# A scan and a two-level expert layer on one core: new ranks for the planner, four weight loads behind the first row load, and three groups of products moved forward

## The chip, the cores and the metric

The kernel runs on one core of one Trainium2 chip. The metric is the device time of one execution in microseconds (us); the time given is the median of three runs. One execution was profiled as well. TensorE is called PE here, VectorE DVE, ScalarE ACT, GpSimd POOL and SyncE SP, as in the profile.

## The reference

The input is 4 sequences of 3648 tokens with 256 channels, 14592 tokens in all. A gated scan runs over each sequence, then each token goes to one of 16 experts, chosen in two levels of 4.

```python
f = lower + (1 - lower) * sigmoid(f_logit)
for t in range(3648):                  # per sequence and channel
    h = f[:, t] * h + (1 - f[:, t]) * x[:, t]
    y[:, t] = h
g = argmax(y @ w_group)                # 4 groups;  g_w = softmax weight of g
e = argmax(y @ w_expert[g])            # 4 experts; e_w = softmax weight of e
out = g_w * e_w * (relu(y @ w1[g, e]) @ w2[g, e])   # 256 -> 1024 -> 256
```

Each token's result is written to its own row of the output.

## The kernel before, in words

**Stages.** The tokens are cut into 29 units of at most 512. A unit's inputs come by one DMA (L499). ACT makes the gates (`tanh` L520, `gate` L530), DVE the inflow (L536) and the scan (L552, one per half `k` of the channels, in order of the units). PE then does three things with the scanned `h`: the router's logits (`router` L608), their turn (`turn` L619), and the rows of the tokens (`back` L562 transposes `h`, ACT takes the high half in L569, `rows_rest` L591 subtracts it on PE, ACT takes the low half in L597). ACT also copies the router's result (`router_out` L614, `logits` L627). 15 groups of one or two units (`GROUPS`) are routed on DVE (L638 to L705) with a few small matmuls on PE (L672 to L689). POOL then scatters the rows, 128 tokens per instruction (L721), into the table `xs`, each expert's rows together.

**Jobs.** 32 jobs do the expert layers: 16 early ones (`EARLY`) on tokens of the first groups, and 16 later ones (`CAPS`) when all ranks are known. A job loads its rows transposed (`job_rows` L944, DMA from `xs` to `x`) and its meta rows (L935, L937), both by SP's queue. Its weights come in four pieces of 512 KB (`job_weights` L953). In the first four jobs (`f2` true) pieces 2 and 3 go straight into their tiles `w2`, `w3`; other pieces go through `st` and are cast by ACT (L959) and DVE (L962). The first products (`m1_mm` L980 to L982) come in groups: for job 0, which has one chunk of 320 columns, eight groups of six matmuls, each group in one PSUM buffer. ACT's relu (L997) empties it; in the first four jobs all groups use the ring `m1` of three buffers (`M1_BUFS`, `TWO_RINGS`). The second product is L1026, its scaling ACT L1037 and DVE L1045, and the way out POOL L1051. A last loop (L1333) takes what is left over.

Job 0 takes rows of groups 0 to 2, that is of 5 units or 20 scatters. Its row load waits until these have landed.

**What sets the order.** The order is not written out. Every step is a task of `Plan` with a key, a cost and the buffers that it takes. `Plan.add` adds to the key a rank out of the table `DELTA`, chosen by a letter and a number: `m3` is the first product of job 3, `r4` the router of unit 4, and so on:

```python
more = float(DELTA.get("%s%d" % self.tag, 0)) if self.tag else 0.0
t.key = key + more
```

`Plan.order` simulates the engines with these keys and returns the list `todo`. A few tasks are moved in the list afterwards, and the program issues the list as it stands, each engine taking its own instructions in that order:

```python
with tc.manual_schedule(engines={ET.SP, ET.PE, ET.DVE, ET.Activation, ET.Pool}):
    for t in todo:
        done = t.fn()
```

So an instruction that waits holds up all that is behind it on its own engine.

Of the kernel before, what the change touches and what calls it, by code (L numbers as in the profile page):

```python
# [49 lines left out]
L_UNIT = 90000.0  # L50
L_RT = 40000.0
L_LOW = 0.0
DELTA = {"B0": -517950, "B8": 43800, "b0": -360450, "b1": -398850, "b2": -500200, "b3": -96200, "b4": -83850, "b5":
# [47 lines left out]
ZX_WAIT = 99000.0  # L101
L_SCAN = 14000.0
L_ZX = 4000.0
# [11 lines left out]
X_BUFS = 5  # L115
HS_BUFS = 2
ROWS_FIRST = 3
BLANKS_FROM = 50000.0
BLANKS_AHEAD = 12000.0

# [176 lines left out]
def gated_scan_moe(ctx: ExitStack, tc, zx, lower, wroute, wexp, out, S):  # L297
# [811 lines left out]
    for g, G in groups.items():  # L1109
        T = G["T"]  # L1110
        key = need[g]
# [136 lines left out]
    tables = A("DVE", 3500, leftovers, after=[put], key=jobs[-13].at)  # L1248
    regs["left"] = None

    for n, j in enumerate(jobs):
        base = j.at
        dep = [T1[member[EARLY[j.nth][1]]]] if j.kind == "A" else [put]
# [3 lines left out]
        for i in range(4):  # L1257
# [3 lines left out]
                   new=[(f"w{i}", n) if i > 1 and j.f2 else ("st", n, i)], size=570000, wait=d - AHEAD)  # L1261
            if i > 1 and j.f2:
                halves[i] = [ld]
                continue
            plan.tag = "p", n
            ha = []
# [16 lines left out]
        for ch in range(len(j.chunks)):  # L1283
            w = j.cw[ch] + j.pad[ch]
            xs_of[ch] = [A("SP", max(1250.0, 15.6 * w / 4), lambda j=j, ch=ch, n=n: job_meta(j) if n < ROWS_FIRST and ch == 0 else job_rows(j, ch),
                          after=rows_dep, key=j.s1[ch] - L_ROWS,
                           new=[("x", n, ch)], size=36000 + int(1550 * w))]
        for ch, (t0, m) in enumerate(j.chunks):
            w = j.cw[ch]
            hb, xb = ("hh", n, ch), ("x", n, ch)  # L1290
# [2 lines left out]
            for cs in j.cols[ch]:  # L1293
                d = j.s1[ch] + cs[0]
                pb = (j.bank[ch, cs[0]], n, ch, cs[0])
                plan.tag = "m", n
                mm = A("PE", len(cs) * 6 * max(w / 2.4 + 2.4, 66.0), lambda j=j, ch=ch, cs=cs: m1_mm(j, ch, cs),
                       after=xs_of[ch] + halves[0] + halves[1], key=d, use=[xb] + wuse, new=[pb])
                hi = A("ACT", 80 + 0.83 * len(cs) * w, lambda j=j, ch=ch, cs=cs: m1_hi(j, ch, cs), after=[mm, firsth], key=d,
                       use=[pb] + ([hb] if firsth else []), new=[] if firsth else [hb])  # L1300
                firsth = firsth or hi
                hidden += [hi, None if j.f2 else A("DVE", 60 + 1.06 * len(cs) * w, lambda j=j, ch=ch, cs=cs: m1_lo(j, ch, cs), after=[hi], key=d,
                                 use=[pb, hb])]
# [14 lines left out]
    for b in [leads[8]] + [t for _, t in commons]:  # L1318
        if b.at > BLANKS_FROM:
            todo.remove(b)  # L1320
            todo.insert(next(i for i, t in enumerate(todo) if t.at >= b.at - BLANKS_AHEAD), b)
    with tc.manual_schedule(engines={ET.SP, ET.PE, ET.DVE, ET.Activation, ET.Pool}):
        for t in todo:
            done = t.fn()
# [76 lines left out]
```

## Time and profile before

| | |
|---|---|
| median of three runs | 729.41 us (727.68 to 730.82) |
| the profiled execution | 728.0 us, span 726.2 us |
| granted TensorE clock, mean of the span | 0.974 |
| PE busy | 689.4 us (95% of the span) |
| DVE, ACT, POOL busy | 506.2 us, 438.8 us, 286.2 us |
| moved by DMA | 151.53 MB, mean 209 GB/s |

The span runs from the first to the last instruction of the profiled execution, and its own time is 1.8 us more. The times of the rows below are counted from the span's start. The granted clock is a share of 2.4 GHz: 0.50 is the level of 1.2 GHz, 1.00 that of 2.4 GHz. PE's matmuls overlap, so the start of one to the start of the next is what it takes; the "us" of a row is from its first start to its last end. A matmul in fp32 leaves two records, so the eight fp32 matmuls of one unit's router stand as sixteen.

### The profile page before, as it was taken

The page shows a single profiled execution, that of the slowest core. Times are in us where ns is not written, and L with a number is a line of the kernel's source. Part 1 is how long each engine was busy: PE and PEld are TensorE (multiplying, and loading weights), DVE is VectorE, ACT ScalarE, POOL GpSimd, SP SyncE. Part 2 cuts the span into 40 slices and gives each one's busy share as a digit, 9 for nine tenths or more (in the row PEclk, how much of TensorE's full clock was granted, in tenths as well). Part 3 has the DMA queues.
Part 4 walks back from the last instruction along what each step waited for, and adds up shares of the span by engine and source line. Part 5 has one row for each costly group of instructions (what it writes and reads, how often), then busy time and mean ns, then how long its engine had stood idle before and what let it go on. Part 6 is the DMA issues. An engine that isn't in the chain of part 4 may idle for free.

```text
span 726.2 us, 17266 instructions
## 1 busy us (share of the span) xinstructions
PE 689.4 (95%) x6480; PEld 570.3 (79%) x6480; DVE 506.2 (70%) x1036; ACT 438.8 (60%) x875; POOL 286.2 (39%) x272
## 2 busy tenths in 40 slices
PE   3757999999999999999999999999999999999995
PEld 1435778788778887887888888899888988888994
DVE  6999599898999968864965532343854427768583
ACT  6987978767795567555445532434654336647572
POOL 1277377676167546472512212222222122143223
PEclk9956999999999999999999999999999999999998
DMA  8899999998988998998388442062767625763750
GB/s 333 315 333 311 341 322 311 305 273 250 346 295 182 322 271 173 243 336 130 94 210 229 142 98 58 30 177 63 183 168 194 142 56 157 225 195 97 266 147 24
DMA packets 133676, 151.53 MB, mean 209 GB/s; under 512 B 103928, under 2 KB 104505, under 8 KB 130263
## 3 DMA queue, kind: packets, MB, share of 16 engines
q1 hardware_dynamic: 120247, 117.19, 58.1%
q0 software_dynamic: 11408, 30.02, 12.6%
q10 hardware_dynamic: 1936, 3.20, 1.9%
q8 instruction: 51, 0.84, 0.5%
q14 instruction: 34, 0.28, 0.1%
HBM read 97.14 MB, written 33.20 MB: 179 GB/s over the span
## 4 chain that ended last, share of the span: by engine, by line
PE 89%; DVE 5%; DMA 2%; ACT 2%; issue 1%; POOL 1%; POOLq 0%; DVEq 0%; ACTq 0%
PE ps_y L1026 42%; PE ps_m L980 8%; PE ps_m L981 7%; PE ps_m L982 7%; PE ps_p L980 6%; PE ps_p L982 6%; PE ps_p L981 6%; DVE h L552 2%; DMA zt<-in_zx_dram 2%; PE ps_p L608 2%; DVE zt L536 1%; PE ps_p L564 1%; DMA lb<-in_lower_dram 1%; ACT zt L520 1%; PE ps_p L562 1%
## 5 line engine op out<-in xcount | busy, mean ns | idle before, releaser
L1026 PE MATMUL ps_y<-w,hh 128*128 128x256 f16 (+11 forms) x3000 | 318.9, 278 | 0.0
L1026 PEld LDWEIGHTS <-hh 128*128 128x128 f16 (+11 forms) x2928 | 252.5, 98 | 33.0 <-issue 4.9
L1051 POOL DMA_INDIRECT out_dram<-o,meta x131 | 143.3, 1094 | 329.9 <-ACT o L1037 263.4
L721 POOL DMA_INDIRECT xs<-rows,posi x114 | 136.5, 1197 | 86.1 <-ACT rows L717 45.1
L962 DVE TENSOR_TENSOR w<-st,w 128x512 bf16<-128x512 f32 (+1 forms) x184 | 149.3, 844 | 30.2 <-ACT w L959 29.9
L1037 ACT ACTIVATE o<-ps_y,meta 128x256 f32<-128x256 f32 (+4 forms) x128 | 60.5, 473 | 156.6 <-PE ps_y L1026 146.4
L959 ACT CAST w<-st 128x512 f16<-128x512 f32 (+1 forms) x184 | 131.5, 747 | 8.8 <-DMA st<-in_wexp_dram 8.6
L980 PE MATMUL ps_m<-x,w 128*128 128x256 f16 (+16 forms) x482 | 131.3, 276 | 0.0
L982 PE MATMUL ps_m<-x,w 128*128 128x256 f16 (+16 forms) x482 | 131.3, 276 | 0.0
L981 PE MATMUL ps_m<-x,w 128*128 128x256 bf16 (+16 forms) x482 | 131.3, 276 | 0.0
L1001 DVE SCALAR_TENSOR_TENSOR hh<-ps_m,hh 128x512 bf16<-128x512 f32 (+12 forms) x130 | 76.4, 590 | 70.3 <-ACT hh L997 69.6
L980 PE MATMUL ps_p<-x,w 128*128 128x256 f16 (+14 forms) x398 | 109.6, 278 | 0.0
L982 PE MATMUL ps_p<-x,w 128*128 128x256 f16 (+14 forms) x398 | 109.5, 278 | 0.0
L981 PE MATMUL ps_p<-x,w 128*128 128x256 bf16 (+14 forms) x398 | 109.5, 278 | 0.0
L997 ACT ACTIVATE hh<-ps_m 128x512 f16<-128x512 f32 (+13 forms) x150 | 78.0, 526 | 42.5 <-PE ps_m L982 34.8
L980 PEld LDWEIGHTS <-w 128*128 128x128 f16 x880 | 86.1, 98 | 20.2 <-issue 4.2
L982 PEld LDWEIGHTS <-w 128*128 128x128 bf16 x880 | 86.1, 98 | 17.5
L981 PEld LDWEIGHTS <-w 128*128 128x128 f16 x880 | 86.1, 98 | 16.5 <-issue 0.2
L1001 DVE SCALAR_TENSOR_TENSOR hh<-ps_p,hh 128x512 bf16<-128x512 f32 (+14 forms) x125 | 74.0, 595 | 19.9 <-ACT hh L997 19.6
L997 ACT ACTIVATE hh<-ps_p 128x512 f16<-128x512 f32 (+14 forms) x125 | 65.9, 527 | 32.7 <-PE ps_p L982 32.3
L552 DVE TENSOR_TENSOR_SCAN h<-zt,h 128x512 f32<-128x512 f32 (+4 forms) x44 | 49.5, 1139 | 0.8 <-PE ps_p L608 0.5
L1045 DVE SCALAR_TENSOR_TENSOR o<-ps_y,meta,o 8x256 f32<-8x256 f32 (+7 forms) x45 | 21.6, 480 | 35.4 <-ACT o L1037 34.2
(152 smaller groups left out, 505.5 us busy)
## 6 DMA issues: line engine op xcount, KB each, us to landing
st<-in_wexp_dram SPq DMA_DIRECT2D x120, 512.0 KB
zt<-in_zx_dram SPq DMA_DIRECT2D x26, 1024.0 KB
w<-in_wexp_dram SPq DMA_DIRECT2D x8, 512.0 KB
zt<-in_zx_dram SPq DMA_DIRECT2D x5, 512.0 KB
out_dram<-o,meta POOLq DMA_INDIRECT x131
xs<-rows,posi POOLq DMA_INDIRECT x114
xs<-blank ACTq DMA_DIRECT2D x1, 1548.0 KB
x<-xs SPq DMA_TRANSPOSE x55
```

What stands on the lines that cost most here:

```text
L552: V.tensor_tensor_scan(out=h[:, k, c0 - a:c1 - a], data0=f[:, c0 - a:c1 - a], data1=x[:, k, c0 - a:c1 - a], initial=init, op0=ALU.mult, op ...
L721: sc = nc.gpsimd.indirect_dma_start(out=xs_v[G["t0"] + t][:, :], out_offset=bass.IndirectOffsetOnAxis(ap=G["posi"][:, t:t + 1], axis=0), i ...
L959: return nc.scalar.copy(j.wh[i][:, at:at + n], j.st[i][:, at:at + n])
L962: V.tensor_tensor(out=j.wl[i][:, at:at + n], in0=j.st[i][:, at:at + n], in1=j.wh[i][:, at:at + n], op=ALU.subtract)
L980: nc.tensor.matmul(po, wh, xh[:, k], start=(k == 0), stop=False)
L981: nc.tensor.matmul(po, wh, xl[:, k], start=False, stop=False)
L982: nc.tensor.matmul(po, wl, xh[:, k], start=False, stop=(k == KD - 1))
L997: return nc.scalar.activation(hi, pv, AF.Relu)
L1001: V.scalar_tensor_tensor(out=lo, in0=pv, scalar=0.0, in1=hi, op0=ALU.max, op1=ALU.subtract)
L1026: nc.tensor.matmul(pm[at:at + p], h[:, c, ts], w[2 + c // 4][:, (c % 4) * D:(c % 4 + 1) * D], start=(i == 0 and m == 0), stop=(i == n - 1 ...
L1037: return nc.scalar.activation(o[0:p], j.pm[ch, t, "y"][0:p], AF.Copy, scale=lt.bitcast(F32)[0:p, r, 1:2])
L1051: last_out[0] = nc.gpsimd.indirect_dma_start(out=out_v[out_n[0]][:, :], out_offset=bass.IndirectOffsetOnAxis(ap=lt[0:p, r, 0:1], axis=0), ...
```

## The change

Three things are changed.

- Every number of `DELTA` is replaced (some 340 of them; no step is added or taken away by that).
- Four weight loads, pieces 2 and 3 of jobs 1 and 2 (512 KB each), are taken out of their place in `todo` and put right behind the task that issues job 0's row load and meta loads.
- The first three groups of job 0's first products are taken out of their place and put ahead of the first task that the plan starts at 64000 ns or later.

The core of the diff (of the table one line of each side is shown):

```diff
-DELTA = {"B0": -517950, "B8": 43800, "b0": -360450, "b1": -398850, "b2": -500200, "b3": -96200, "b4": -83850, "b5":
...
+DELTA = {"B0": -544500, "B8": 45200, "b0": -497500, "b1": -490500, "b2": -724600, "b4": -193200, "b5": 48600, "b6":
...
+FIRST_AT = 64000.0
...
+    behind = []
+    first_rows, first_mm = [], []
     for n, j in enumerate(jobs):
...
             if i > 1 and j.f2:
                 halves[i] = [ld]
+                if n in (1, 2):
+                    behind.append(ld)
                 continue
...
+        first_rows.append(xs_of[0])
...
+                if n == 0:
+                    first_mm.append(mm)
...
+    behind.sort(key=lambda t: t.at)
+    for t in behind:
+        todo.remove(t)
+    at = todo.index(first_rows[0][0]) + 1
+    todo[at:at] = behind
+    for t in first_mm[:3]:
+        todo.remove(t)
+    at = next(i for i, t in enumerate(todo) if t.at >= FIRST_AT)
+    todo[at:at] = first_mm[:3]
     with tc.manual_schedule(engines={ET.SP, ET.PE, ET.DVE, ET.Activation, ET.Pool}):
```

**SP, around job 0's row load.** Before, the four loads into `w` stand ahead of the row load (L944):

```order
L499 DMA zt<-in_zx_dram 128x2048
L953 DMA w_756<-in_wexp_dram 128x1024
L953 DMA w_773<-in_wexp_dram 128x1024
L953 DMA w_828<-in_wexp_dram 128x1024
L953 DMA w_844<-in_wexp_dram 128x1024
L916 TENSOR_LOAD posa_641
...
L944 DMA_TRANSPOSE x<-xs 128x4x320
...
L935 DMA meta<-xs 128x2x2
...
L937 DMA meta<-xs 64x2
L499 DMA zt<-in_zx_dram 128x2048 x4
```

Now:

```order
L499 DMA zt<-in_zx_dram 128x2048
L916 TENSOR_LOAD posa_643
...
L944 DMA_TRANSPOSE x<-xs 128x4x320
...
L935 DMA meta<-xs 128x2x2
...
L937 DMA meta<-xs 64x2
L953 DMA w_879<-in_wexp_dram 128x1024
L953 DMA w_881<-in_wexp_dram 128x1024
L953 DMA w_883<-in_wexp_dram 128x1024
L953 DMA w_885<-in_wexp_dram 128x1024
L499 DMA zt<-in_zx_dram 128x2048 x4
```

The four loads have gone from in front of the row load to between it and the next four loads of inputs; the rest of this piece stands as it did.

**PE, around the router of unit 8.** `rows_853` (now `rows_845`) are the rows of unit 7, `h_867` (now `h_859`) is the scanned unit 8, and `ps_m1` is a buffer of a group of job 0's first products. Before:

```order
L591 MATMUL ps_p_848<-rows_853,minus_133 128x256
L608 MATMUL ps_p_893<-h_867,wr_90 32x128 x8
L562 MATMUL ps_p_902<-ident_76,h_867 128x128 x4
L619 MATMUL ps_p_913<-ident_76,rs_910 128x128
L562 MATMUL ps_p_915<-ident_76,h_867 128x128 x4
...
L591 MATMUL ps_p_915<-rows_920,minus_133 128x256
L980 LDWEIGHTS w0_348
L980 MATMUL ps_m1_940<-x_878,w0_348 128x320
...
L982 MATMUL ps_m1_940<-x_878,w1_436 128x320
L562 MATMUL ps_p_953<-ident_76,h_891 128x128 x4
```

Now:

```order
L591 MATMUL ps_p_840<-rows_845,minus_133 128x256
L980 LDWEIGHTS w0_353
L980 MATMUL ps_m1_888<-x_870,w0_353 128x320
...
L980 MATMUL ps_m1_895<-x_870,w0_353 128x320
...
L980 MATMUL ps_m1_902<-x_870,w0_353 128x320
...
L608 MATMUL ps_p_914<-h_859,wr_90 32x128 x8
L562 MATMUL ps_p_923<-ident_76,h_859 128x128 x4
L619 MATMUL ps_p_934<-ident_76,rs_931 128x128
L562 MATMUL ps_p_936<-ident_76,h_859 128x128 x4
```

All three groups, 18 matmuls, stand now between unit 7's last row product and unit 8's router. Before, one group stood behind unit 8's row products and the next two farther on, among those of units 9 and 10.

**ACT, in the same place.** Here is what ACT has now; before, the same steps stood in the same order:

```order
L597 CAST rows_845<-ps_p_840 128x2x256
L614 COPY rs_931<-ps_p_914 128x128
L569 CAST rows_941<-ps_p_923 128x2x256
L627 COPY Lg_851<-ps_p_934 128x80
L569 CAST rows_941<-ps_p_936 128x2x256
L597 CAST rows_941<-ps_p_923 128x2x256
L597 CAST rows_941<-ps_p_936 128x2x256
L645 ACTIVATE ex_963<-ge_959 128x160
L710 COPY pay_965<-tokno_125 128x8
L997 ACTIVATE hh_972<-ps_m1_888 128x320
L569 CAST rows_991<-ps_p_967 128x2x256
```

So the relu of the first group (L997, `ps_m1_888`) has stayed behind the whole of unit 8's rows, and its copy of the router (L614) is still the next thing behind unit 7's rows.

## Rows read from the trace of the kernel before

**Rows 1.** the page: busy time and share of each engine; the chain that ended last

```profile
PE 689.4 (95%) x6480; PEld 570.3 (79%) x6480; DVE 506.2 (70%) x1036; ACT 438.8 (60%) x875; POOL 286.2 (39%) x272
...
PE 89%; DVE 5%; DMA 2%; ACT 2%; issue 1%; POOL 1%; POOLq 0%; DVEq 0%; ACTq 0%
```

**Rows 2.** stretches: start:end, length, busy us of PE to POOL, clock, DMA share, GB/s

```profile
49.00:63.00 14.00, 9.42 (x60) 6.68 (x61) 13.01 (x29) 12.02 (x26) 11.54 (x9) 0.62 1.02 403
61.00:65.33 4.33, 3.78 (x21) 2.52 (x21) 4.29 (x5) 3.43 (x9) 3.72 (x3) 0.50 0.85 319
64.00:67.00 3.00, 1.73 (x13) 0.49 (x11) 2.96 (x3) 1.66 (x3) 2.28 (x3) 0.50 0.58 131
67.00:69.00 2.00, 1.77 (x14) 1.39 (x15) 2.00 (x3) 0.30 (x2) 1.80 (x1) 0.50 1.27 280
67.23:70.67 3.44, 3.19 (x20) 2.42 (x20) 3.44 (x4) 1.62 (x5) 2.87 (x2) 0.51 1.13 245
70.67:85.00 14.33, 14.26 (x126) 10.68 (x126) 7.48 (x27) 13.92 (x34) 2.67 (x3) 1.00 1.04 332
85.00:400.00 315.00, 314.93 (x2790) 256.23 (x2789) 261.04 (x493) 206.67 (x403) 170.68 (x150) 1.00 0.93 254
400.00:719.00 319.00, 318.91 (x3290) 278.37 (x3288) 175.46 (x340) 160.67 (x326) 76.94 (x75) 1.00 0.49 137
```

**Rows 3.** PE's waits from 60 to 719 us: total us, times, longest

```profile
PE ps_p L608 <- DVE h L552: 2.3, 3, 1.0
PE ps_p L608 <- ACT rows L597: 1.5, 1, 1.5
PE ps_p L591 <- ACT rows L569: 0.5, 2, 0.2
```

**Rows 4.** timeline of PE: start, us, line, tiles, count [idle before <-releaser]

```profile
64.74 0.59 PE L591 MATMUL ps_p<-rows,minus 128*128 128x256 f16 x2 [0.25 <-ACT rows L569]
66.09 0.66 PE L608 MATMUL ps_p<-h,wr 128*32 128x128 f32 x8 [0.77 <-DVE h L552]
67.23 0.66 PE L608 MATMUL ps_p<-h,wr 128*32 128x128 f32 x8 [0.48 <-DVE h L552]
67.81 1.12 PE L562 MATMUL ps_p<-ident,h 128*128 128x128 f32 x4
...
70.89 0.30 PE L980 MATMUL ps_m<-x,w 128*128 128x320 f16 x1
...
71.70 1.48 PE L562 MATMUL ps_p<-ident,h 128*128 128x128 f32 x12
...
77.68 0.27 PE L619 MATMUL ps_p<-ident,rs 128*128 128x128 f32 x1
...
82.59 3.62 PE L1026 MATMUL ps_y<-w,hh 128*128 128x256 f32 x16
```

**Rows 5.** timeline of ACT around unit 8's rows

```profile
67.95 0.27 ACT L614 COPY rs<-ps_p 128x128 f32<-128x128 f32 x1 [2.00 <-PE ps_p L608]
68.97 0.59 ACT L569 CAST rows<-ps_p 128x512 f16<-128x512 f32 x1 [0.75 <-PE ps_p L562]
...
70.03 0.58 ACT L569 CAST rows<-ps_p 128x512 f16<-128x512 f32 x1 [0.35 <-PE ps_p L562]
...
76.94 0.35 ACT L614 COPY rs<-ps_p 128x128 f32<-128x128 f32 x1
...
78.05 1.06 ACT L520 ACTIVATE zt<-zt 128x1024 f32<-128x1024 f32 x1 [0.41 <-DMA zt<-in_zx_dram]
```

**Rows 6.** timeline of SP around job 0's row load

```profile
49.46 2.83 SPq L953 DMA_DIRECT2D w<-in_wexp_dram  x4
64.26 1.47 SPq L944 DMA_TRANSPOSE x<-xs  x1
...
67.32 5.50 SPq L499 DMA_DIRECT2D zt<-in_zx_dram  x4
```

**Rows 7.** timeline of POOL, the twentieth scatter

```profile
58.16 0.97 POOL L721 DMA_INDIRECT xs<-rows,posi  x1 [0.31 <-issue]
```

93 rows, old and new, of the table DELTA are left out of this document.

## The prediction

> **What bounds the kernel now.** I read four views in this order. First the page's busy shares and the chain that ended last: PE is busy 95% of the span and holds 89% of the chain [rows 1], so the time is PE's time unless something keeps PE waiting or cold. Then the busy time of stretches [rows 2]: from 70.67 us to 719 us PE is busy 14.26 of 14.33, 314.93 of 315 and 318.91 of 319 us at a granted clock of 1.00. That leaves 0.23 us of idle time in 648 us. Ahead of 70.67 it is another kernel: from 61 to 65.33 us and from 67.23 to 70.67 us the clock is 0.50 and 0.51, the level of 1.2 GHz, and DVE is busy all the time. Third PE's waits from 60 us on: 2.3 us for the scan, 1.5 and 0.5 us for ACT's row copies [rows 3], the whole of what the change can find there. Last the timelines of the engines around 65 us [rows 4 to 7], for the place that it touches.
>
> **New ranks, from 85 us on.** PE has the same instructions in another order. Since it has 0.23 us of idle time and the full clock, a better order can give nothing there; a worse one can open a wait. DVE (261 of 315 us) and ACT (207 of 315 us) have room, and more of it behind 400 us [rows 2]. Bounds: 0 below, for nothing is left to gain; above, the longest single wait since 60 us, 1.5 us [rows 3], for each wait that opens. I take 0, the nearest row being the stretch itself. The cover is that room; where it is gone the price is R2 below.
>
> **Four weight loads moved.** Four pieces of 512 KB are 2.1 MB. From 49 to 63 us the DMA engines are full (share 1.02) at 403 GB/s [rows 2]; at that rate the four take 5.2 us of the 14. They are issued at 49.46 us, the twentieth scatter starts at 58.16 us, and the row load that waits for it starts at 64.26 us [rows 6, 7]. With the loads out of the way that scatter lands earlier. Ends: 59.1 us (the scatter's own 0.97 us over) and 64.3 us (nothing gained). I take 61.5 us, near the middle, since no row shows the queue without them.
>
> When is `x` there? No row shows its landing. From 64 to 67 us the DMA moves 131 GB/s, from 67 to 69 us 280 GB/s [rows 2]; I take the slow 3 us for the row load and get 64.5 us. Ends: 62.1 and 67.3 us by the same 3 us, and 70.89 us as the latest, since the first product then ran [rows 4]. PE comes to the moved products when unit 7's last row product is over, 64.74 + 0.59 = 65.33 us, so in the forecast they do not wait.
>
> SP's order behind the row load: meta loads, the four weights, then the four input loads, which stood at 67.32 us [rows 6]. Row load and meta loads took 3.06 us of SP, the weights 2.83 us: 61.5 + 5.9 = 67.4 us, the same issue time. But 5.2 us of transfers now lie ahead of them. Before, the second of the inputs landed as ACT's tanh at 78.05 us, which had waited 0.41 us for it [rows 5]; that is 13.8 us after the row load's start. Adding 5.2 and taking off the idle share of 64 to 67 us (0.42 of 3 us, 1.3) gives 17.7 us, or 79.2 us: 1.15 us late. With the row load at 59.1 us it is 1.2 us early, at 64.3 us 4 us late.
>
> The Trainium skill, page "DMA: Bandwidth & Descriptors", section "Queues, rings and completion order", says that a DMA engine goes round between the queues that hold work, packet by packet. By that a scatter on POOL's queue never stood behind all of SP's weights, only shared with them. Taking them away would then bring less than 5.2 us, and the row load would stay nearer to 64 us. The 5.1 us from the scatter's end to the row load [rows 6, 7] do not decide it. What it would make of the sum is R1 below.
>
> **Three groups of products moved.** Six matmuls take 71.70 - 70.89 = 0.81 us at full clock [rows 4], so 18 take 2.43 us, and 4.86 us at half. They start at 65.33 us, into 0.77 + 0.48 us of idle time before and between the two halves of unit 8's router (66.09 and 67.23 us) [rows 4]. Before, the clock rose after a stretch that PE filled from 67.23 us on. Now the filled stretch begins 1.9 us earlier, so I let the clock rise 1.9 us earlier, at 68.8 us: 13 of the 18 at half clock (3.5 us), five at full (0.7 us), over at 69.5 us. The whole router then takes about 0.66 us at full clock (half of it took as long at half clock): 70.15 us, where it ended at 67.23 + 0.66 = 67.89 us before. So ACT's copy L614 starts 2.26 us later than its 67.95 us [rows 5].
>
> ACT is the point, because its order has not changed: the relu of the first group still stands behind all of unit 8's copies. While PE does the products ACT waits, as it did for 2.00 us before [rows 5], and now for longer. Something comes back: at half clock the transposes took 1.12 us per four [rows 4], so ACT's two copies L569 stood 1.02 and 1.06 us behind what was before them [rows 5]. At full clock I take 0.50 and 0.59 us (a copy's own time), which returns 1.0 us. ACT is then 1.25 us late, and from 70.67 to 85 us it is busy 13.92 of 14.33 us [rows 2], so it can't catch up. At its copy of unit 9's router (76.94 us, over at 77.29) PE had 0.39 us in hand, for its turn L619 ran at 77.68 us [rows 4, 5]. So PE is 0.86 us late there, with the same work done as before at that point. The late input adds at most its 1.15 us to the same chain, not on top. I take 0.9 us for the start of the second product (82.59 us before) [rows 4], and all behind it moves by as much.
>
> Bounds of this part: with full clock from 65.33 us the router ends at 65.33 + 2.43 + 0.66 = 68.42 us, 0.53 us late, and 1.0 us comes back: -0.5 us. With half clock throughout it ends at 65.33 + 4.86 + 1.32 = 71.5 us, 3.6 us late with nothing back, less 0.39 us and the 0.41 us for the input: +2.8 us. A gain larger than 0.5 us is excluded as long as ACT's order holds.
>
> The Trainium skill, page "TensorE: Matmul & The Clock Gate", section "Part 4: PE-mode transpose", says that transposes on PE do not count as busy in the same way for the clock. The row of 67.23 to 70.67 us, where eight of the transposes L562 run, has 0.51, and the rise came right behind it, so it leaves both readings open. By the rule, 18 plain products in a row would raise the clock sooner than I let them: the sum would be nearer the lower bound.
>
> **Sum.** 0 (ranks) + 0 (row load in time) + 0.9 (ACT's chain) = +0.9 us on the profiled execution's 728.0 us, so 728.9. That execution lies 1.4 us under the median of 729.41 us; the same step on the median gives 730.3 us.
>
> **Rivals.**
> - R1, slower: the row load is no earlier. `x` then comes at 67.3 us and the router waits 2.0 us more; the input lands 4 us late, so ACT's tanh starts at 82.0 instead of 78.05 us. The larger of 2.0 + 0.9 and 3.95 sets it, about +4: 733.4. It decides from a row load behind 63 us. For it: 5.1 us between scatter and row load that no row divides. Against: full DMA queues exactly in that stretch [rows 2].
> - R2, slower: the new order opens waits in the fed stretch. Three of the 1.5 us of [rows 3] are +4.5: 733.9. Against: the room of DVE and ACT.
> - R3, no change: full clock from the first moved product, -0.5 us: 728.9. For it: a row of 18 products without a gap. Against: the half clock from 61 to 65.33 us, though PE was busy 3.78 of 4.33 us there [rows 2].
> - R4, faster: ACT does not hold PE back, and the idle time and the half clock of 65.33 to 70.89 us both go: 0.77 + 0.48 + 0.24 us (the last of it in the 0.5 of [rows 3]) and half of the about 4.07 us that PE was busy (5.56 - 1.49), 2.0: -3.5. With some of the earlier waits gone too it is -4: 725.4. Against: ACT's unchanged order and its full 14 us.
> - The change does what it says in the order of SP and PE; that it has no effect there is no case of its own.
>
> **How the numbers follow.** A measurement of this kernel can tell about 0.5%, 3.65 us, from no change: the edges are 725.76 and 733.06 us. Forecast 0.48, R1 0.18, R2 0.08, R3 0.14, R4 0.12. Slower by over 0.5%: two thirds of R1 and of R2 and a little of the forecast (the half clock throughout), 0.19. Faster: most of R4, 0.10. Within: 0.71. The range of 727.0 to 733.9 us takes in R3, the forecast with its bounds and R1, and leaves out R4 and what of R2 is dearer than three waits.
>
> **What would show it.** Right: the row load at 60 to 63 us; 18 products in a row from about 65.3 us, without a wait; L614 of unit 8 near 70 us; a new idle time of ACT ahead of it and of PE between 71 and 80 us, for ACT's copies; the second product at about 83.5 us; from 85 us on PE without a wait. Wrong: a wait of the first product for `x`, or a tanh that waits 3 us for its input (R1); waits of PE behind 85 us (R2); the second product at or before 82.1 us (R3, R4); a clock of 0.50 again behind 71 us, which I have not priced beyond the bound of +2.8.

## The result: slower by 6.7 us, and the profile after

| | before | after |
|---|---|---|
| median, same chip, 6 runs each | 729.84 us (727.68 to 731.13) | 736.52 us (734.15 to 738.46) |
| ratio | | 1.0092 (95%: 1.0063 to 1.0122) |
| the profiled execution | 728.0 us, span 726.2 us | 734.75 us, span 733.0 us |
| granted clock, mean | 0.974 | 0.964 |

The forecast was 730.3 us with a range of 727.0 to 733.9 us; the result lies outside it. The two profiled executions differ by as much as the medians (6.75 us), so their traces can be set against each other. The kernel before takes about 729 us on some chips and 741 to 746 us on others; so every kernel below stands against the kernel before on its own chip, and sizes in us are read on the chips of 729 us.

The page of the changed kernel, busy times and the chain that ended last:

```profile
PE 691.7 (94%) x6480; PEld 570.7 (78%) x6480; DVE 506.7 (69%) x1036; ACT 437.8 (60%) x875; POOL 287.7 (39%) x272
...
PE 82%; DMA 7%; DVE 3%; ACT 3%; SPq 2%; issue 2%; POOL 1%; POOLq 0%; ACTq 0%
```

PE's work is the same; DMA went from 2% to 7% of the chain and PE from 89% to 82% [rows 1]. Two marks on PE split the loss. The first second-layer product (L1026) stood at 82.59 us [rows 4] and stands at 85.93 us, so 3.34 us are lost in the head. The last one went from 716.13 to 722.88 us, 6.75 us late; so 3.4 us more are lost in the stretch that was fed without a gap before [rows 2]. Three PE rows of that stretch carry a wait (start, us, line, tiles, count, idle before and its releaser):

```profile
254.64 0.33 PE L619 MATMUL ps_p<-ident,rs 128*128 128x128 f32 x1 [0.47 <-ACT rs L614]
...
267.01 0.27 PE L980 MATMUL ps_m<-x,w 128*128 128x256 f16 x1 [0.50 <-DMA x<-xs]
...
575.92 0.28 PE L980 MATMUL ps_m<-x,w 128*128 128x256 f16 x1 [2.23 <-DMA x<-xs]
```

They sum to 3.20 us; with the head's 3.34 that is 6.54 of the 6.75 us.

**The head.** PE's timeline after, around the moved products and then where PE stops:

```profile
64.28 0.59 PE L591 MATMUL ps_p<-rows,minus 128*128 128x256 f16 x2 [0.25 <-ACT rows L569]
64.94 0.43 PE L980 MATMUL ps_m<-x,w 128*128 128x320 f16 x1
...
65.69 0.44 PE L980 MATMUL ps_m<-x,w 128*128 128x320 f16 x1
65.96 0.31 PE L981 MATMUL ps_m<-x,w 128*128 128x320 bf16 x1
66.11 0.30 PE L982 MATMUL ps_m<-x,w 128*128 128x320 f16 x1
...
67.96 0.65 PE L608 MATMUL ps_p<-h,wr 128*32 128x128 f32 x16
...
74.94 0.65 PE L608 MATMUL ps_p<-h,wr 128*32 128x128 f32 x16
...
78.60 0.38 PE L591 MATMUL ps_p<-rows,minus 128*128 128x256 f16 x2 [2.10 <-ACT rows L569]
79.25 0.33 PE L619 MATMUL ps_p<-ident,rs 128*128 128x128 f32 x1 [0.28 <-ACT rs L614]
...
82.15 0.47 PE L982 MATMUL ps_m<-x,w 128*128 128x320 f16 x1
...
85.93 3.62 PE L1026 MATMUL ps_y<-w,hh 128*128 128x256 f32 x16
```

Job 0's row load is issued at 60.67 us, 3.6 us earlier than before [rows 6] (row below). The 18 products run from 64.94 us without a wait for `x`, and from one start to the next it is 0.27 us up to 65.96 us and 0.14 us behind it: the clock rises there, 2.8 us sooner than forecast. At 74.94 us PE is ahead of before, where this router stood at 75.25 us, and has 18 of the 48 first products behind it instead of 12. Then it does six more products and stands still for 2.10 us, for a row copy of ACT. SP's row load, then ACT's timeline, then the chain of waits over the same place, say why:

```profile
60.67 1.70 SPq L944 DMA_TRANSPOSE x<-xs  x1
```

```profile
68.67 0.27 ACT L614 COPY rs<-ps_p 128x128 f32<-128x128 f32 x1 [3.18 <-PE ps_p L608]
...
77.02 1.06 ACT L520 ACTIVATE zt<-zt 128x1024 f32<-128x1024 f32 x1 [2.11 <-DMA zt<-in_zx_dram]
77.98 0.57 ACT L569 CAST rows<-ps_p 128x512 f16<-128x512 f32 x1
...
79.51 1.06 ACT L520 ACTIVATE zt<-zt 128x1024 f32<-128x1024 f32 x1
```

```profile
63.89 0.57 SPq L953
...
66.53 10.46 DMA zt<-in_zx_dram
77.04 0.94 issue
77.98 0.57 ACT rows L569
```

The router's copy L614 is only 0.72 us later than before [rows 5], and by its last relu (74.41 us, before 74.72 us) ACT has made that up. ACT waits for the *first* of the four inputs, which stand behind the moved weights on SP's queue and land 10.5 us after their issue; the second tanh, at 79.51 us, waits for nothing. Single microseconds of the same place (start:end, length, busy us of PE, PEld, DVE, ACT, POOL, granted clock, DMA share, GB/s):

```profile
76.00:77.00 1.00, 0.50 (x4) 0.23 (x3) 0.00 (x0) 0.00 (x0) 0.00 (x0) 1.00 1.03 434
77.00:78.00 1.00, 0.00 (x0) 0.00 (x0) 0.00 (x0) 0.98 (x2) 0.00 (x0) 1.00 0.99 418
78.00:79.00 1.00, 0.38 (x2) 0.10 (x1) 0.00 (x0) 1.00 (x4) 0.00 (x0) 1.00 1.08 442
79.00:80.00 1.00, 0.74 (x4) 0.51 (x5) 0.00 (x0) 1.00 (x4) 0.00 (x0) 0.81 0.97 393
80.00:81.00 1.00, 1.00 (x5) 0.61 (x4) 0.00 (x0) 1.00 (x3) 0.00 (x0) 0.50 1.00 418
...
82.00:83.00 1.00, 1.00 (x7) 0.37 (x5) 0.00 (x0) 0.34 (x2) 0.00 (x0) 0.50 1.02 418
```

The DMA engines are full in all of these rows (share 0.97 to 1.08), and the stop costs twice: behind it the clock is 0.50 until 83 us. The bill of the head: PE was 0.31 us ahead at the router and had six products more done (0.81 us), so 1.12 us in hand. It lost 2.10 + 0.28 + 0.16 (at 83.61 us) = 2.54 us to waits. The twelve products from 79.42 us took 3.00 us instead of 1.63, which is 1.4 us, and the small matmuls behind them 0.89 instead of 0.58 us, another 0.3 us; some 0.2 us more lie in short gaps between the matmuls. 2.54 + 1.9 - 1.12 = 3.3 us.

That fall of the clock belongs to this execution. At the same place PE waits 1.25 us in `after_3` (the same kernel once more), 1.65 us in `moves_only_3` and 1.82 us in `x_first`, and the clock stays at 1.00 up to 83 us; their first L1026 stands at 84.42 to 84.77 us. In `after_3` what that saves is lost again at the next job: before, PE came to its first product at 86.04 us; in the profiled execution of the changed kernel it is 89.39 us, without a wait, and in `after_3` 90.27 us, behind one of 2.23 us.

**The late wait.** SP's rows from 546 us on, of the kernel before and then of the changed one (start, us, line, tiles, count):

```profile
546.56 0.93 SPq L953 DMA_DIRECT2D st<-in_wexp_dram  x2
550.16 1.27 SPq L944 DMA_TRANSPOSE x<-xs  x1
562.94 0.34 SPq L953 DMA_DIRECT2D st<-in_wexp_dram  x1
563.48 5.10 SPq L944 DMA_TRANSPOSE x<-xs  x1
```

```profile
546.46 20.44 SPq L953 DMA_DIRECT2D st<-in_wexp_dram  x5
567.10 7.88 SPq L944 DMA_TRANSPOSE x<-xs  x2
```

Before, the first row load of job 21 went out at 550.16 us, ahead of the last weight piece of job 23. With the new ranks it stands behind that piece, and the piece waits for its `st` buffer, which DVE frees with a cast, as SP's waits from 540 to 600 us show (line, what it waited for, us, times, longest):

```profile
SPq L953 <- DVE w L962: 17.2, 1, 17.2
```

So the row load goes out at 567.10 us, `x` comes 8.8 us later, and PE stands 2.23 us for it.

### The profile page after: what moved, and what is told of

It reads as the page before. It is cut to its first block, busy times and chain, and to the rows that moved or that the text cites. A ratio compares the mean times of both kernels' runs of the same rounds, so it can differ in the third digit from the quotient of the medians.

```text
span 733.0 us, 17260 instructions
## 1 busy us (share of the span) xinstructions
PE 691.7 (94%) x6480; PEld 570.7 (78%) x6480; DVE 506.7 (69%) x1036; ACT 437.8 (60%) x875; POOL 287.7 (39%) x272
## 4 chain that ended last, share of the span: by engine, by line
PE 82%; DMA 7%; DVE 3%; ACT 3%; SPq 2%; issue 2%; POOL 1%; POOLq 0%; ACTq 0%
PE ps_y L1026 40%; PE ps_m L980 7%; PE ps_m L982 7%; PE ps_m L981 7%; PE ps_p L980 6%; PE ps_p L981 6%; PE ps_p L982 6%; DMA x<-xs 2%; DMA zt<-in_zx_dram 2%; PE ps_p L608 1%; DMA st<-in_wexp_dram 1%; DVE h L552 1%; PE ps_p L564 1%; SPq L587 1%; DMA lb<-in_lower_dram 1%
## 5 line engine op out<-in xcount | busy, mean ns | idle before, releaser
L1026 PE MATMUL ps_y<-w,hh 128*128 128x256 f16 (+10 forms) x3000 | 319.0, 278 | 0.0
L1026 PEld LDWEIGHTS <-hh 128*128 128x128 f16 (+11 forms) x2928 | 252.5, 98 | 32.9 <-issue 5.2
L1051 POOL DMA_INDIRECT out_dram<-o,meta x131 | 139.8, 1068 | 327.2 <-ACT o L1037 259.8
L721 POOL DMA_INDIRECT xs<-rows,posi x114 | 142.3, 1248 | 94.1 <-ACT rows L717 40.4
L997 ACT ACTIVATE hh<-ps_m 128x512 f16<-128x512 f32 (+13 forms) x150 | 78.1, 524 | 55.0 <-PE ps_m L982 34.4
L997 ACT ACTIVATE hh<-ps_p 128x512 f16<-128x512 f32 (+14 forms) x125 | 65.9, 528 | 31.2 <-PE ps_p L982 30.0
```

What stands on the lines that cost most here:

```text
L721: sc = nc.gpsimd.indirect_dma_start(out=xs_v[G["t0"] + t][:, :], out_offset=bass.IndirectOffsetOnAxis(ap=G["posi"][:, t:t + 1], axis=0), i ...
L997: return nc.scalar.activation(hi, pv, AF.Relu)
L1026: nc.tensor.matmul(pm[at:at + p], h[:, c, ts], w[2 + c // 4][:, (c % 4) * D:(c % 4 + 1) * D], start=(i == 0 and m == 0), stop=(i == n - 1 ...
L1051: last_out[0] = nc.gpsimd.indirect_dma_start(out=out_v[out_n[0]][:, :], out_offset=bass.IndirectOffsetOnAxis(ap=lt[0:p, r, 0:1], axis=0), ...
```

## The experiments

All kernels below compute the whole output. Each undoes or adds one part, but for `weights_move_only`, which came out as `moves_only` once more. The diffs are shortened, and "..." marks what is left out. The table gives the ratio to the kernel before on the same chip, the start of the first L1026, and PE's waits for `x` (us) at three places; "old" and "new" are the ranks.

| kernel, ranks | chip | median us | ratio (95%) | L1026 | near 90 | 235-270 | 570-595 |
|---|---|---|---|---|---|---|---|
| ranks_only, new | 8 | 749.9 | 1.0119 (1.0083-1.0155) | 84.03 | 0.15 | 0.98 | 2.37 |
| moves_only, old | 8 | 742.72 | 1.0022 (0.9996-1.0049) | 87.70 | 0 | 0 | 0 |
| no_products_move, new | 8 | 751.43 | 1.0128 (1.0091-1.0166) | 86.60 | 0 | 0 | 2.62 |
| moves_inputs_first, old | 8 | 748.04 | 1.0075 (1.0045-1.0105) | 87.55 | 3.95 | 0 | 0 |
| before_again, old | 3 | 739.99 | before itself | 85.01 | 1.12 | 0 | 0 |
| after_again, new | 3 | 751.19 | 1.0118 (1.0062-1.0175) | 84.73 | 2.44 | 1.15 | 2.39 |
| moves_only_2, old | 3 | 743.49 | 1.0019 (0.9985-1.0054) | 84.03 | 1.81 | 0 | 0 |
| ranks_only_2, new | 3 | 751.77 | 1.0138 (1.0068-1.0208) | 83.93 | 0 | 0.87 | 2.37 |
| x_first, new | 7 | 739.0 | 1.0133 (1.0102-1.0164) | 84.47 | 1.75 | 1.00 | 2.07 |
| inputs_first, new | 7 | 740.69 | 1.0138 (1.0107-1.0168) | 82.52 | 5.69 | 0.91 | 2.07 |
| both_fixes, new | 7 | 739.29 | 1.0137 (1.0118-1.0155) | 82.55 | 4.77 | 0.92 | 2.14 |
| products_move_only, old | 7 | 734.71 | 1.0073 (1.0059-1.0086) | 89.30 | 0 | 0 | 0 |
| after_3, new | 1 | 736.49 | 1.0086 (1.0069-1.0102) | 84.42 | 2.23 | 0.95 | 2.30 |
| x21_first, new | 1 | 733.76 | 1.0068 (1.0043-1.0093) | 84.53 | 1.89 | 0.90 | 0 |
| ranks_only_3, new | 1 | 735.48 | 1.0085 (1.0065-1.0105) | 82.66 | 1.63 | 0 | 2.06 |
| moves_only_3, old | 1 | 731.03 | 1.0031 (1.0017-1.0045) | 84.77 | 0.65 | 0 | 0 |
| ranks_x21, new | 13 | 748.35 | 1.0015 (0.9979-1.0051) | 83.30 | 1.36 | 1.07 | 0 |
| weights_move_only (in fact moves_only), old | 13 | 744.43 | 0.9988 (0.9958-1.0019) | 85.96 | 0 | 0.26 | 0 |

### Ranks and moves apart

`ranks_only` has the new table and none of the moves; `moves_only` has the old table and both moves.

```diff
 # ranks_only: DELTA as after
-    for t in behind: ...          # the four weights stay in their place
-    for t in first_mm[:3]: ...    # the products stay in theirs
 # moves_only: both blocks kept
-DELTA = (new)
+DELTA = (old)
```

> The new ranks alone: the four weight loads and the three groups of products stay where the planner puts them. Theory A (two separate losses: the weights ahead of the inputs cost 3.3 us up to the first second product, the new ranks cost 3.2 us in two waits of PE for x): about 3.2 us slower than before, 733.0; the first L1026 at about 82.6 us; PE waits of about 2.2 us for x near 570 us and 1 us near 255 to 267 us. Theory B (all of it comes from the ranks): 6.7 us slower. Theory C (the waits near 255 and 570 us follow from the late head): no change, no wait of PE behind 100 us.

> The two moves with the old ranks. Theory A: about 3.3 us slower, 733.1; tanh waits some 2 us for its input near 77 us, PE waits some 2 us behind it, the clock falls, the first L1026 at about 85.9 us; no wait of PE behind 100 us. Theory B: no change. Theory C: 6.7 us slower, with waits for x behind 200 us.

> The new ranks alone, a second time. Theory A: 3.2 us slower, the first L1026 within 1 us of before, PE waits for x of 1 us near 260 us and 2.2 us near 573 us. Theory C: no change and no such wait.

> The two moves with the old ranks, a second time. Theory A: 3.3 us slower, the first L1026 3.3 us later than before, all of it behind a tanh that waits 2 us for its input; no wait of PE for x near 573 us. Theory C (the later waits follow from the late head): those waits come here too, 6.7 us slower. Theory F (what the first try showed, a delay of all engines between 45 and 56 us with no releaser in the trace, belongs to the old ranks with the moves): the same delay again, unit 7's copy L614 at 65 us or later.

> The new ranks alone. On a chip of about 729 us, theory A: 3 to 5 us slower (the first L1026 at 82.6 us as before, waits of PE for x of 1 us near 236 to 267 us and 2.1 us near 574 us, and up to 1.6 us for a fall of the clock). If the ranks alone carry the whole loss: 6.7 us or more.

> The two moves with the old ranks. On a chip of about 729 us, theory A: 2 to 4 us slower, all of it ahead of 100 us (late input for tanh near 77 us, perhaps a wait for job 1's x near 90 us); no wait of PE for x behind 100 us. If the ranks alone carry the loss: no change.

On three chips the ranks alone cost 0.85% to 1.4%, and every interval lies clear of no change. The moves alone cost 0.2% to 0.3% there, and nothing on a fourth (0.9988, in the row of `weights_move_only`, whose kernel is the same); only the interval of chip 1 lies clear of no change. On chip 1 (729.4 us before) that is +6.1 us and +1.6 us, and together (`after_3`) +7.1 us; that the parts sum to 0.6 us more is within the intervals. The larger part is the one that I had put at nothing. On the chips of 741 us and more the head says little: in `moves_only` PE stands still for 4.14 and 2.63 us between 44 and 54 us and DVE for 2.40 us ahead of 56.76 us, stops that the profile puts down to nothing in the kernel, and its first L1026 is late for that. `moves_only_2` missed its expectation: its tanh has no wait in the head, and its first L1026 is not later than that of `before_again` but 0.98 us earlier. The late input is thus shown with the old ranks by one profile, `moves_only_3`.

PE's waits behind 85 us in `ranks_only_3`, then in `moves_only_3`:

```profile
PE ps_m L980 <- DMA x<-xs: 3.7, 2, 2.1
PE ps_p L619 <- ACT rs L614: 1.0, 1, 1.0
```

```profile
PE ps_m L980 <- DMA x<-xs: 0.6, 1, 0.6
```

The ranks open the waits behind 100 us, and without a late head: the first L1026 of `ranks_only_3` stands at 82.66 us. Its last one is 5.21 us later than before (721.34 against 716.13 us), of which the waits behind 85 us are 4.7 us: 1.63 us near 88, 1.01 near 254 and 2.06 near 574 us. So in that execution, of 733.26 us, the waits are nearly the whole loss; its median is 2.2 us longer, and for that there is no trace. The moves open the wait in the head: `moves_only_3` has the tanh's wait of 1.67 us for the first input, PE's 1.65 us behind it, and its first L1026 2.18 us late. Its first moved product also waits for `x`, and runs at full clock from its start (the next one follows after 0.13 us):

```profile
66.58 0.30 PE L980 MATMUL ps_m<-x,w 128*128 128x320 f16 x1 [1.20 <-DMA x<-xs]
```

### Is it the weights or the products, in the head?

`no_products_move` has the new ranks and the weights' move; the products stay where the plan puts them. `products_move_only` has the old ranks and the products' move. `weights_move_only` was to have the old ranks and the weights' move.

```diff
 # no_products_move: against after
-    for t in first_mm[:3]: ...
 # products_move_only: against before
+    for t in first_mm[:3]: ...
 # weights_move_only: against before, the same edit as moves_only
+    for t in behind: ...
+    for t in first_mm[:3]: ...
```

> The new kernel, but with the three groups of products where the planner puts them; new ranks and the move of the weights stay. Theory A (in the head the weights ahead of the inputs are the cause): still 6 us or more slower, 736; tanh still waits for its input near 77 us and the first L1026 is not before 85 us. Theory D (in the head the moved products are the cause, by ACT's copies behind them): about 3.2 us slower, 733, the first L1026 at about 82.6 us.

> The old ranks, the weight loads where they were, and only the three groups of products moved. My prediction's chain (ACT waits for the router behind the products): the router's copy of unit 8 some 2 us later than before and the first L1026 0.9 us later, 0.1% slower; if x is not there in time (the row load at 64 us as before), PE waits 1 to 3 us for it ahead of the products and the first L1026 comes 2 to 5 us later.

> The old ranks, the products where they were, only the four weight loads behind the first row load. Theory A (the moved bytes, not the moved products, cost the head): tanh waits 1.5 to 2.3 us for its input near 77 us, the first L1026 1.5 to 3 us later than before, 1.5 to 3.5 us slower in all. Theory D (the products and ACT's order): no change, the first L1026 at 82.6 us or earlier.

Without the moved products the input is as late. The first tanh in `no_products_move`:

```profile
78.12 1.06 ACT L520 ACTIVATE zt<-zt 128x1024 f32<-128x1024 f32 x1 [2.32 <-DMA zt<-in_zx_dram]
```

The first L1026 stands 2.6 us behind that of `ranks_only` on the same chip, which differs by the weights' move alone and has no such wait. So with the new ranks the weights are the cause of the late input, and not the products. The products need the weights out of the way all the same, as PE's timeline of `products_move_only` shows:

```profile
70.20 0.42 PE L980 MATMUL ps_m<-x,w 128*128 128x320 f16 x1 [4.74 <-DMA x<-xs]
```

There the row load is issued at 64.41 us, as before, and `x` is not there for 4.74 us. `weights_move_only` does not answer its question: the kernel that ran has the products' move as well, and its trace shows the first product ahead of unit 8's router:

```profile
68.81 0.47 PE L980 MATMUL ps_m<-x,w 128*128 128x320 f16 x1
...
72.01 0.64 PE L608 MATMUL ps_p<-h,wr 128*32 128x128 f32 x16
```

It is a fourth run of `moves_only`. The weights' move alone, with the old ranks, was not tried.

### Can the inputs go first?

`moves_inputs_first` (old ranks) and `inputs_first` (new ones) put the four weights behind the four inputs:

```diff
-    at = todo.index(first_rows[0][0]) + 1
+    at = todo.index(first_rows[0][0])
+    at = [i for i, t in enumerate(todo)
+          if i > at and t.eng == "SP" and t.new and t.new[0][0] == "zt"][3] + 1
```

> The two moves with the old ranks, but the four weight loads stand behind the four input loads, not ahead of them. Theory A: the loss of the head goes; no wait of tanh for an input between 70 and 82 us, no half clock behind 70 us, the first L1026 at 81.7 to 82.6 us, the time 0 to 1 us under before (728.9 to 729.9). Theory D: 1 to 3 us slower than before, the same as with the weights first.

> The new kernel, with the four weight loads behind the four input loads. Theory A (the weights ahead of the inputs make the tanh wait): no wait of tanh for an input near 77 us and the first L1026 at 82 to 83.5 us, 2.5 to 3.5 us less than the new kernel. Theory D (the moved products and ACT's order make it): the first L1026 stays at 85 to 86 us.

The wait for the input goes, and the first L1026 of `inputs_first` is at 82.52 us, as early as before. But the sum is no better: `inputs_first` takes 740.69 us where `x_first`, the nearest to the changed kernel on that chip, takes 739.0 us, and `moves_inputs_first` 748.04 us where `moves_only` takes 742.72 us. PE then stands at the next job's first product:

```profile
82.52 3.62 PE L1026 MATMUL ps_y<-w,hh 128*128 128x256 f32 x16
91.83 0.37 PE L980 MATMUL ps_m<-x,w 128*128 128x256 f16 x1 [5.69 <-DMA x<-xs]
```

Its row load now stands behind the weights. From 64 to 83 us the DMA engines of the changed kernel are busy by a share of 0.97 and so have no room for 2.1 MB more; of the two orders tried each made another load late.

### The late wait

`x_first` takes one row load out of its place ahead of a weight piece, and `x21_first` another; `both_fixes` is `x_first` with the inputs first; `ranks_x21` is the ranks alone with the edit of `x21_first`.

```diff
 # x_first:   job 23's row load ahead of that job's piece 0
 # x21_first: job 21's first row load ahead of job 23's piece 3
+    rows21 = first("x", 21, 0)
+    todo.remove(rows21)
+    todo.insert(todo.index(first("st", 23, 3)), rows21)
```

> The new kernel, with one row load (x of job 23, first chunk) issued ahead of the first weight piece of the same job instead of behind it, as the old ranks had it. Theory A (SP's order makes the late wait: the piece waits some 17 us for its buffer and the row load stands behind it): the wait of PE for x near 573 to 592 us goes, 2.2 to 2.4 us less than the new kernel. Theory G (the transfer itself is slow there, whatever the order): the wait stays, no change against the new kernel.

> The new kernel with both edits: row load of job 23 ahead of its weight piece, and the four weight loads behind the four input loads. Theory A on a chip of about 729 us: within 1 us of before, 728 to 730.5. If the ranks lose in other places too, as the chips of about 741 us suggest: 5 us or more above before.

> The new kernel, with the row load of job 21 (first chunk) ahead of the last weight piece of job 23, where the old ranks had it. My try with job 23's row load moved the wrong one: in its trace the load that PE waits for near 576 us is job 21's. Theory A: the wait near 574 us goes, and with it 2 to 4 us (2.1 us of waiting and what a fall of the clock behind it costs). Theory G (the transfer is late whatever the order): no change against the new kernel.

> The new ranks alone, with job 21's row load ahead of the last weight piece of job 23. Theory A: no wait of PE near 574 us; what is left of the ranks' loss are waits of 1 us near 236 to 254 us and 0 to 1.6 us near 88 us: 1 to 4 us slower than before on a chip of about 729 us. Rival: the ranks cost 6 us for another reason that the trace's waits don't show, and still do.

In `x_first` I had moved the wrong load. Its wait stayed, 2.07 us at 576.02 us, and SP's rows were those of the changed kernel; `both_fixes`, which moves the same load, keeps the wait too (2.14 us). With the right one the wait is gone. SP in `x21_first`:

```profile
546.83 2.71 SPq L953 DMA_DIRECT2D st<-in_wexp_dram  x4
554.88 1.29 SPq L944 DMA_TRANSPOSE x<-xs  x1
566.94 0.34 SPq L953 DMA_DIRECT2D st<-in_wexp_dram  x1
567.67 5.10 SPq L944 DMA_TRANSPOSE x<-xs  x1
```

The order of before is back, PE is busy 50.00 of the 50 us from 550 us on (47.70 in `after_3`, at a clock of 0.97), and the median is 2.7 us lower than that of `after_3` on the same chip (733.76 against 736.49). That size is loose, since the executions of the two overlap (732.52 to 736.81 and 735.18 to 739.81 us); that the wait goes is plain. The wait of 2.06 to 2.62 us stands in all ten profiles that have the new ranks without this edit, and in none of the eight with the old ranks nor the two with the edit. `ranks_x21` lies at 1.0015, where the ranks alone have 1.0085 to 1.0138; it ran on another chip than those, so its size is a hint and no more. No kernel beat the one before.

### The same kernels again

> The kernel before once more, for a trace on the same chip as the next three: 728 to 743 us, whichever chip it is; on a chip of about 729 us the first L1026 at 82.6 us and no wait of PE behind 100 us, on one of about 741 us waits of PE between 90 and 400 us.

> The new kernel once more. All theories: 6 to 9 us slower than before on the same chip. Theory A: the first L1026 3.3 us later than before, and PE waits for x of 1 us near 260 us and 2.2 us near 573 us.

> The new kernel a third time, beside the next three. On a chip of about 729 us: 6 to 9 us slower; tanh waits about 2 us for its input near 77 us, the first L1026 at 84.5 to 86 us, PE waits for x near 90 us (0 to 2 us), near 236 to 267 us (1 us) and near 574 us (2.1 us).

These tell what belongs to the change and what may not. The wait near 90 us is not the change's alone: `before_again` has it, and so have kernels with either ranks. But on the chips of 729 us it is 1.63 to 2.23 us in `x_first`, `after_3`, `x21_first` and `ranks_only_3`, none in the first profile of the changed kernel, and 0.65 us or none in the three with the old ranks; so whether the ranks make it longer is open. (In `inputs_first` and `both_fixes` the order adds to it, as said above.) The load is the second of the two row loads behind the head. Before, it was issued at 81.88 us and PE came to its product at 86.04 us without a wait, so it landed in at most 4.16 us. The chain of waits of `ranks_only_3` shows the same load, at the same place in the order:

```profile
82.32 5.55 DMA x<-xs
```

That load takes 5.55 us here, 6.46 us in `after_3` and at most 4.16 us before, so the same kernel shows the wait in one profile and not in another.

## Why the prediction was wrong, step by step

- **"New ranks: I take 0" is the step that failed.** PE's 0.23 us of idle time and the room of DVE and ACT were true and not to the point. The cover that I named does not reach the waits that opened: most are for row loads, and what a row load waits for is SP's queue, of which I had read the rows around the first row load alone. One swap on it, which a program order of before and after shows, cost 2.1 to 2.3 us on the chips of 729 us. R2 had the place and the kind (a wait in the fed stretch, 1.5 us each) at a chance of 0.08; three waits of 3.2 us in all came, and 6.1 us by the medians with the ranks alone. What of the 6.1 is more than the swap I can only divide in part. With the new ranks `x` is 0.9 to 1.2 us late near 240 us in nine of twelve profiles. A wait of 0.5 to 1.0 us for ACT stands near 254 us in two, but on another chip the old ranks have it too (2.62 us in `moves_only`, at 264.03 us). The wait near 90 us and the clock that sometimes falls behind a wait may add to it. Why those waits come, and the 2.2 us between the profiled execution and the median of `ranks_only_3`, stay open.
- **"Row load in time, 0": right in the profile of the change.** The row load came at 60.67 us against a forecast of 61.5 us, and `x` was there at 64.94 us. R1 falls. In `moves_only_3` the first product still waited 1.20 us for `x`. By the Trainium skill's rule of queues served in turn (page "DMA: Bandwidth & Descriptors", section "Queues, rings and completion order") I had let R1 keep the row load near 64 us; it came 3.6 us earlier than before, of the 5.2 us that the four loads take, so what I had drawn from the rule did not come true. Nor does the trace show that sharing set the limit to the gain: the twentieth scatter, from 57.70 us, took 2.78 us to land, and from 58 to 61 us the DMA engines were busy by a share of 0.38 to 0.40 only.
- **"0.9 us on ACT's chain": the sign right by luck, the term mis-sized (3.3 us to the first L1026), and by another way.** ACT's chain hardly moved, since the clock rose at 65.96 and not at 68.8 us: L614 was 0.72 us late and not 2.26, and ACT came to its last relu ahead of the wait at 74.41 us. For an earlier rise I had named the Trainium skill, page "TensorE: Matmul & The Clock Gate", section "Part 4: PE-mode transpose", by which I let plain products bring it. The runs do not bear that out as the reason: in `moves_only_3` the clock is 1.00 from 65 to 66 us, ahead of the first moved product at 66.58 us. What cost instead was the input. I priced the second of the four, because that one had a wait before [rows 5]; my 79.2 us for it is not tested, since its tanh at 79.51 us waited for nothing. The first had no wait before, so no row showed it, and I took that for room. It had none: its tanh waited 2.11 us. By the medians of chip 1 the moves alone cost 1.6 us.
- **Half clock again behind 71 us** was named as what I had not priced. It came in that profile (0.50 from 80 to 83 us) and cost about 1.7 of the head's 3.3 us; it stayed away at that place in `after_3`.
- R4 falls: the idle time and the half clock ahead of 70.89 us did go (PE was 1.12 us ahead at 74.94 us), and were lost again within 8 us. R3's sign was wrong for the same reason.

## What to carry to other kernels

Where an issuing queue is in order, look in the new order for every load that is passed by one which waits for a buffer: that makes the load late by the whole wait (17.2 us here, of which PE felt 2.23), whatever room the engines have. A load whose consumer shows no wait may have no time in hand; before you put bytes ahead of it, work out its landing from the issue and the rate, as for the one that does wait. And bytes that leave one full stretch of the DMA engines go into another; ask first whether that one is full as well.

## What the runs showed of the hardware

- A wait of PE of some 2 us is followed by half clock at some times and not at others. In the changed kernel the clock is 0.50 behind the 2.10 us at 78.60 us, and stays at 1.00 around the 2.23 us at 575.92 us (first row); in `after_3` it is 0.66 in the 5 us behind a wait of 2.23 us at 90.27 us (second row). No run here tells why.

```profile
570.00:582.00 12.00, 9.77 (x92) 8.47 (x90) 2.16 (x7) 1.43 (x3) 0.98 (x1) 1.00 0.86 177
```

```profile
90.00:95.00 5.00, 4.73 (x29) 3.61 (x29) 3.17 (x4) 2.99 (x5) 4.09 (x4) 0.66 0.99 394
```

- The same kernel before took 729 us on chips 1 and 7, 741 us on 3 and 8, and 746 us on 13. Where it is slower, the profile shows stops that it puts down to nothing in the kernel, among them one of PE of 5.00 us ahead of 49.53 us in `before_again`. What they are was not tried.
- In the changed kernel a load of 1 MB (the first of the four inputs) behind 2.1 MB on the same queue landed 10.5 us after its issue; from 76 to 83 us, around and behind its landing, the rows shown have 393 to 442 GB/s.
